# Four tiles of a normalised input transposed by DMA from ScalarE's queue in place of TensorE

## The chip, the core and the metric

The kernel runs on one core of a Trainium2 chip. The metric is the device time of one execution in microseconds (us). Engine names: PE is TensorE's matrix multiply and PEld its loading of weights, DVE is VectorE, ACT is ScalarE, POOL is GpSimd, SP is SyncE. SPq, ACTq and POOLq are the instruction streams from which these engines issue DMAs; each has a DMA queue of its own (in the DMA rows q1 is that of SP, q10 that of ACT, q0 that of POOL), and all of them use the same 16 DMA engines.

## What is computed

The input x has 2048 rows of 640 values in bf16. It is normalised row by row, and two branches of the normalised xn are added to x.

```
xn  = (x - mean(x)) / sqrt(var(x) + 1e-5)            # per row
q, k, v = xn @ wqkv                                  # 640 -> 3 x 640, 32 heads of 20
logits[s, w] = q[s] . k[s - 2 w] * 20**-0.5          # w = 0..7, masked where s - 2 w < 0
o   = softmax(logits) weighted sum of v[s - 2 w]
h   = (xn @ w_gate) * (xn @ w_up)                    # 640 -> 1536
out = x + o @ wo + h @ w_down
```

## The kernel before, in words

The rows are cut into 16 tiles of 128 rows, and four tiles make one of four chunks (`CH = 4`). In a chunk the matmuls take 512 rows at once. TensorE needs xn with the 640 features on the partitions, so each tile of xn is transposed once: `xnT` of a chunk is 128 x 5 x 512, with two buffers for the four chunks.

**Loading and normalising.** `load_x` (L163 to L167) loads one tile of x into one of five buffers. `ln` (L277 to L283) adds the steps of a tile: two halves of statistics on VectorE (L252), the mean and variance (L258, L260), the reciprocal root on GpSimd (L266), and the normalisation in place on VectorE (L271). The list `turn` in `ln` makes the statistics of tiles 0 to 4 wait for an earlier tile's normalisation, so that VectorE finishes tiles in turn there.

**Transposing.** `transposes` (L300 to L330) has two ways. Tiles under `XDMA = 8` are transposed by TensorE, five 128 x 128 blocks into PSUM (L310), and copied to xnT by ScalarE (L314). Tiles 8 to 15 are transposed by a DMA from SBUF to SBUF, issued by SP (L318). As soon as a tile is transposed, its buffer is free, so `transposes` also adds the load of x tile t + 5. Tiles 5 to 7 are loaded by SP, tiles 8 to 12 by ScalarE, tiles 13 to 15 by GpSimd.

**Products.** `qk` (L347 to L368) computes q and k of a chunk, ten groups of five matmuls of 128 x 512 (L355), each group in one PSUM bank that ScalarE evicts (L362). `vproj` computes v of one tile in two halves (L381, evicted at L387, stored at L398 to `vD` in DRAM). `load_v8` (L486) reads `vD` back with the eight shifted rows for each row. `prodlog` multiplies q with shifted k on VectorE, eight products of 128 x 2560 per chunk (L415) in five buffers, sums them by head on TensorE in two groups (L425), and evicts and transposes the logits (L438, L446, issued by SP). `softmax` and `av` are VectorE's (L460 to L527), and their output tile is transposed by an SP DMA (L534). `glu` computes gate and up (L551, evicted at L556, multiplied by VectorE at L567), `down` computes the output (L589, L592), added to x at L598.

**Order.** The kernel is planned before it is built. Each step is added with an engine, a cost in us and the steps it depends on. `Plan.order` walks all engines in time, and of the steps that are ready on an engine takes the one that is due first, counted back from the end. The result is one fixed list of instructions for each engine, and an engine does its list strictly in order. `after` is a dependence on the start of a step only, `occ` the time in which a step holds its engine, `floor` an earliest end, `margin` a delay added ahead of a step's start, and `kb` the size of a transfer that queues behind others on SP. The main matmuls, TensorE's transposes among them, form a chain through `pe_main` (L288 to L295): each comes after the one before, and after the eviction of the bank six places earlier (`ring`). The weights are loaded by SP in the order wv, wq, wk, wg, wu (`load`), then v of tile 0 and wd (`load_v8`, `load_down`).

At the place of the change, TensorE's order is written out by hand (L642 to L650): the five groups of q of chunk 0, the transposes of tiles 4 and 5, the five groups of k of chunk 0, the transposes of tiles 6 and 7, v of tile 3, and then (L673 to L676) q and k of chunk 1 and v of tiles 4 to 7. q and k of chunk 1 need `TT[4]` to `TT[7]`, the four tiles of chunk 1's xnT.

Of the kernel before, what the change touches and what calls it, by code (L numbers as in the profile page):

```python
# [9 lines left out]
ACT = mybir.ActivationFunctionType  # L10
# [21 lines left out]
class Plan:  # L32
# [8 lines left out]
    def add(self, eng, cost, fn, deps=(), occ=None, after=(), kb=0):  # L41
        s = Step(eng, cost, fn, deps, occ, after)
        s.kb = kb
        s.idx = len(self.steps)
        self.steps.append(s)
        return s
# [51 lines left out]
def kernel(  # L98
# [11 lines left out]
    nc = tc.nc  # L110
    P = nc.NUM_PARTITIONS
# [13 lines left out]
    NT = S // P  # L125
    CH = 4
# [27 lines left out]
    add = plan.add  # L154
    T = {}

    def new(key, shape, dtype, tag, bufs, pool=None):
        t = (pool or sb).tile(shape, dtype, name=tag, tag=tag, bufs=bufs)
        T[key] = t
        return t  # L160


    def load_x(t, eng=None):  # L163
        def fn():
            x = new(("x", t), [P, D], BF, "x", 5)
            (eng or nc.sync).dma_start(out=x[:], in_=x_flat[t * P : (t + 1) * P, :])  # L166
        return fn  # L167

    X = {}

    def wload(dst, src, eng=None):
        return lambda: (eng or nc.sync).dma_start(out=dst[:], in_=src.rearrange("(i p) f -> p i f", p=P))
# [9 lines left out]
    def load(at, fn, deps=()):  # L182
        s = chain[0] = add("SP", 2.0, fn, deps, occ=0.45, after=[chain[0]])
        s.floor = at
        return s
# [62 lines left out]
    def ln_stats(t, g):  # L248
        def fn():
            if g == 0:  # L250
                new(("st", t), [P, 2, nc.vector.BN_STATS_DIM], F32, "st", 3)
            nc.vector.bn_stats(T["st", t][:, g, :], T["x", t][:, g * NS : (g + 1) * NS])  # L252
        return fn

    def ln_aggr(t):
        def fn():
            mv = new(("mv", t), [P, nc.vector.BN_AGGR_DIM], F32, "mv", 6)
            nc.vector.bn_aggr(mv[:], T["st", t][:])  # L258
            ve = new(("ve", t), [P, 1], F32, "ve", 6)
            nc.vector.tensor_scalar(ve[:], mv[:, 1:2], scalar1=EPS, scalar2=None, op0=ALU.add)  # L260
        return fn

    def ln_rstd(t):
        def fn():
            rs = new(("rstd", t), [P, 1], F32, "rstd", 6)
            nc.gpsimd.tensor_tensor(rs[:], T["ve", t][:], mhalf[:], ALU.pow)  # L266
        return fn

    def ln_apply(t):
        def fn():  # L270
            nc.vector.tensor_scalar(T["x", t][:], T["x", t][:], scalar1=T["mv", t][:, 0:1],  # L271
                                    scalar2=T["rstd", t][:], op0=ALU.subtract, op1=ALU.mult)
        return fn

    XT, TT, GL, RS = {}, {}, {}, {}

    def ln(t):  # L277
        turn = [XT.get(t - (2 if t < CH else 1)), GL.get(t - 1)] if t <= CH else []
        a = add("DVE", 0.48, ln_stats(t, 0), [X[t], GL.get(t - 3), *turn], occ=0.395)
        a = add("DVE", 0.48, ln_stats(t, 1), [a], occ=0.395)  # L280
        a = GL[t] = add("DVE", 0.39, ln_aggr(t), [a], occ=0.3)
        b = RS[t] = add("POOL", 0.56, ln_rstd(t), [a])
        XT[t] = add("DVE", 0.443, ln_apply(t), [b], occ=0.35)  # L283
# [4 lines left out]
    def pe_main(cost, fn, deps=(), banks=1):  # L288
        nonlocal main
        waits = []  # L290
        for k in range(banks):
            if len(ring) + k >= 6:
                waits.append(ring[len(ring) + k - 6])
        main = add("PE", cost + 0.165, fn, [main, *waits, *deps], occ=cost)
        return main  # L295

    XDMA = 8
    GP = {}

    def transposes(t):  # L300
        c, q = divmod(t, CH)

        def slot():
            if q == 0:
                new(("xnT", c), [P, KT, CS], BF, "xnT", 2)

        def pe():
            ps = new(("pst", t), [P, KT, P], BF, "ps", 6, psum)
            for g in range(KT):
                nc.tensor.transpose(ps[:, g, :], T["x", t][:, g * P : (g + 1) * P], ident[:])  # L310

        def ev():
            slot()
            nc.scalar.copy(T["xnT", c][:, :, q * P : (q + 1) * P], T["pst", t][:])  # L314

        def dma():
            slot()
            nc.sync.dma_start_transpose(out=T["xnT", c][:, :, q * P : (q + 1) * P], in_=T["x", t][:])  # L318

        if t < XDMA:  # L320
            a = pe_main(0.28, pe, [XT[t]])
            TT[t] = add("ACT", 0.695, ev, [a], occ=0.6)
            ring.append(TT[t])
        else:
            a = TT[t] = add("SP", 2.8, dma, [XT[t], GP.get(c - 2)], occ=1.28, kb=200)
        if t + 5 < W:
            X[t + 5] = load(11.9 + 0.45 * t, load_x(t + 5), [a])
        elif t + 5 < NT:
            e, dge = ("ACT", nc.scalar) if t < XDMA else ("POOL", nc.gpsimd)
            X[t + 5] = add(e, 6.0, load_x(t + 5, dge), [a], occ=0.45, kb=0 if t < XDMA else 160)  # L330

    Q, Kk, LASTPW = {}, {}, {}
    HALOCP = {}

    def halo(c):
# [68 lines left out]
    SPLAST = [None]  # L404
    PW, LL, LE, SS, DD, AA, O16, OE, V8, DT = {}, {}, {}, {}, {}, {}, {}, {}, {}, {}

    def prodlog(c):
        for g in range(2):
            n = 2 * c + g
            for j in range(4):  # L410
                i = 4 * g + j

                def mul(i=i):
                    p = new(("pw", c, i), [P, KT, CS], BF, "pw", 5)
                    nc.vector.tensor_tensor(p[:], T["q", c][:], T["k", c][:, :, DIL * i : DIL * i + CS], ALU.mult)  # L415

                m = 8 * c + i
                PW[m] = add("DVE", 1.48, mul, [*Q[c], *Kk[c], LL.get((m - 5) // 4) if m >= 5 else None], occ=1.395)
            LASTPW[c] = PW[m]

            def lg(g=g):
                l = new(("lps", c, g), [P, 512], F32, "pl", 2, psum)
                for i in range(KT):
                    for j in range(4):
                        nc.tensor.matmul(l[H * j : H * (j + 1), :], lhsT=Ek[:, i, :], rhs=T["pw", c, 4 * g + j][:, i, :],  # L425
                                         start=(i == 0), stop=(i == KT - 1), tile_position=(0, H * j),
                                         skip_group_check=True)

            LL[n] = add("PE", 1.28, lg, [*[PW[8 * c + 4 * g + j] for j in range(4)], LE.get(n - 2), CE], occ=1.195)
            LL[n].urgent = True  # L430
            LL[n].margin = 1.0

            def ev(g=g):
                L = new(("L", c, g), [P, CS], BF, "L", 2)
                if c == 0:
                    ps = T["lps", c, g]
                    nc.vector.tensor_tensor(ps[:, 0:HALO], ps[:, 0:HALO], negm[:, g, :], ALU.add)
                nc.scalar.copy(L[:], T["lps", c, g][:])  # L438

            LE[n] = add("ACT", 0.585, ev, [LL[n], SS.get(n - 2), CM], occ=0.5)  # L440

            def tr(g=g):
                if g == 0:
                    new(("LT", c), [P, CH, W, H], BF, "LT", 1)
                out = T["LT", c][:].rearrange("p t (g w) h -> p t g (w h)", g=2)[:, :, g, :]
                nc.sync.dma_start_transpose(out=out, in_=T["L", c, g][:])  # L446

            early = [SPLAST[0]] if c == 0 else []
            SS[n] = SPLAST[0] = add("SP", 3.5, tr, [LE[n], DD.get(2 * c - 1), DD.get(2 * c - 2)], occ=1.25, after=early, kb=160)
            if c == 0 and g == 0:  # L450
                load_v8(1)
                SPLAST[0] = V8[1]
# [46 lines left out]
    def load_down():  # L499
        WL["d"] = SPLAST[0] = add("SP", 8, wload(wd, B_w_down), after=[SPLAST[0]], occ=0.5, kb=1920)  # L500

    def load_out():
        WL["o"] = SPLAST[0] = add("SP", 8, wo_load, after=[SPLAST[0]], occ=2.7, kb=1100)
# [121 lines left out]
    for t in range(4):  # L625
        ln(t)
# [3 lines left out]
    transposes(0)  # L630
    vproj(0, (0,))
    transposes(1)
    vproj(0, (1,))
    vproj(1, (0,))
# [5 lines left out]
    WL["g"] = load(17.2, wload(wg, B_w_gate))  # L640
    WL["u"] = load(23.2, wload(wu, B_w_up))
    qk(0, 0, CS, (0,))  # L642
    for t in (4, 5):
        ln(t)
        transposes(t)
    qk(0, 0, CS, (1,))
    for t in (6, 7):
        ln(t)
        transposes(t)
    vproj(3)  # L650
# [8 lines left out]
    def attention(c):  # L659
        if c == 0:  # L660
            SPLAST[0] = WL["u"]
            load_v8(0)
            load_down()
        prodlog(c)
        if c == 0:
            load_out()
            load_v8(2)
        for hf in range(2):
            softmax(c, hf)
        for q in range(CH):  # L670
            av(c * CH + q)
# [47 lines left out]
```

## Time and profile before

| | us |
|---|---|
| median of 3 runs | 269.42 (269.28 to 270.31) |
| the profiled execution | 269.1 |
| its span | 267.4 |
| PE busy | 260.2 (97%) |
| DVE busy | 215.2 (80%) |
| ACT busy | 108.6 (41%) |
| POOL busy | 40.7 (15%) |

The span runs from the first instruction to the last; 1.7 us of the profiled execution lie around it. Busy is the time in which an engine had at least one instruction of its own in work. A chain is followed back from the last instruction: at each step to what released it, or to the instruction before it on its engine. A row of a timeline gives the start, the length, the engine and line, what is written from what, how many instructions the row takes together, and in brackets the idle time ahead of it with what ended it. A row of DMA packets gives the queue, the number of packets, the megabytes, and the time of these packets as a share of the 16 DMA engines in the stretch that was asked for; packets in flight overlap, so a share can be over 100%. A landing is counted from the start of a DMA's issue.

### The profile page before, as it was taken

To read this page: it belongs to the slowest core of one execution; us is meant where nothing else is said; L and a number is where in the kernel's file an instruction comes from. 1 tells how busy PE (TensorE), PEld (TensorE's weight loads), DVE (VectorE), ACT (ScalarE), POOL (GpSimd) and SP (SyncE) were. 2 spreads that over 40 slices of the span, in tenths; PEclk is the share of its full clock that TensorE was granted. 3 is DMA by queue.
4 is the path that set the end of the run, shared out by engine and by line. 5 is a ranking of instruction groups with operands and counts; after the bars stand their busy time and mean duration, and the time that the engine had idled before them with its cause. 6 is when DMAs were issued, how large, how long until landed. Compare 5 with 4: busy or idle time off the path is not lost.

```text
span 267.4 us, 4130 instructions
## 1 busy us (share of the span) xinstructions
PE 260.2 (97%) x1596; PEld 141.7 (53%) x1596; DVE 215.2 (80%) x334; ACT 108.6 (41%) x197; POOL 40.7 (15%) x84
## 2 busy tenths in 40 slices
PE   7799999999999999999999999999999999999994
PEld 2545446444477645544456754644447764445772
DVE  4673999999999999999992999999829999931221
ACT  2657555655500066555520125655552005554000
POOL 4540006400003220500000010330000104000000
PEclk9999999999999999999999999999999999999999
DMA  6999977995497192995137947395029178110001
GB/s 217 356 390 398 367 186 248 252 232 146 110 285 173 44 319 101 241 343 81 25 61 103 298 170 222 89 331 50 20 45 368 57 241 150 25 25 0 27 31 43
DMA packets 47235, 45.89 MB, mean 172 GB/s; under 512 B 21954, under 2 KB 44368, under 8 KB 47216
## 3 DMA queue, kind: packets, MB, share of 16 engines
q1 hardware_dynamic: 43696, 36.28, 48.9%
q0 software_dynamic: 2384, 8.05, 9.4%
q10 hardware_dynamic: 1136, 1.31, 1.4%
q8 instruction: 12, 0.20, 0.4%
q14 instruction: 7, 0.06, 0.1%
HBM read 35.39 MB, written 5.26 MB: 152 GB/s over the span
## 4 chain that ended last, share of the span: by engine, by line
PE 95%; DMA 2%; ACT 1%; SPq 0%; issue 0%; DVE 0%; ACTq 0%
PE ps L551 39%; PE ps L589 20%; PE ps L355 16%; PE ps L592 8%; PE ps L381 8%; PE pl L425 4%; DMA wv<-in_A_wqkv_dram 2%; ACT xnT L314 1%; PE ps L310 0%; ACT v_t L387 0%; SPq L166 0%; DVE xr L598 0%; ACTq L166 0%; ACTq L387 0%
## 5 line engine op out<-in xcount | busy, mean ns | idle before, releaser
L551 PE MATMUL ps<-xnT,wg 128*128 128x512 bf16 x240 | 59.7, 379 | 0.0
L551 PE MATMUL ps<-xnT,wu 128*128 128x512 bf16 x240 | 59.7, 379 | 0.0
L589 PE MATMUL ps<-wd,hT 128*128 128x320 bf16 x384 | 57.4, 299 | 0.0
L415 DVE TENSOR_TENSOR pw<-q,k 128x2560 bf16<-128x2560 bf16 x32 | 46.4, 1485 | 2.2 <-ACT k L362 2.1
L589 PEld LDWEIGHTS <-hT 128*128 128x128 bf16 x384 | 37.4, 98 | 15.9 <-issue 0.8
L512 DVE TENSOR_TENSOR v<-v,a 128x5120 bf16<-128x5120 bf16 x16 | 45.1, 2819 | 0.1
L556 ACT CAST gs<-ps 128x512 bf16<-128x512 f32 x48 | 28.1, 586 | 40.7 <-PE ps L551 40.7
L551 PEld LDWEIGHTS <-wu 128*128 128x128 bf16 x240 | 23.3, 98 | 28.7 <-issue 0.8
L551 PEld LDWEIGHTS <-wg 128*128 128x128 bf16 x240 | 23.3, 98 | 28.1 <-issue 0.8
L556 ACT CAST us<-ps 128x512 bf16<-128x512 f32 x48 | 28.1, 586 | 23.3 <-PE ps L551 22.7
L567 DVE TENSOR_TENSOR hT<-gs,us 128x512 bf16<-128x512 bf16 x48 | 19.8, 420 | 14.4 <-ACT us L556 14.2
L598 DVE TENSOR_TENSOR xr<-ps,xr 128x320 bf16<-128x320 f32 x32 | 14.8, 485 | 19.4 <-PE ps L592 15.6
L592 PE MATMUL ps<-wo,oT 128*128 128x320 bf16 x160 | 27.0, 299 | 0.0
L620 POOL DMA_DIRECT2D out_dram<-xr x14 | 7.7, 548 | 123.0 <-DVE xr L598 123.0
L381 PE MATMUL ps<-wv,xnT 128*128 128x320 bf16 x160 | 23.6, 299 | 1.4 <-DMA wv<-in_A_wqkv_dram 1.1
L521 DVE TENSOR_TENSOR v<-v 128x2560 bf16<-128x2560 bf16 x16 | 23.8, 1485 | 0.1
L355 PE MATMUL ps<-xnT,wq 128*128 128x512 bf16 x100 | 22.2, 379 | 0.2 <-ACT xnT L314 0.2
L355 PE MATMUL ps<-xnT,wk 128*128 128x512 bf16 x100 | 22.4, 379 | 0.0
L381 PEld LDWEIGHTS <-xnT 128*128 128x128 bf16 x160 | 15.2, 98 | 8.5 <-ACT xnT L314 1.9
L592 PEld LDWEIGHTS <-oT 128*128 128x128 bf16 x160 | 15.7, 98 | 6.1
L252 DVE BATCH_NORM_STATS2 st<-x 128x6 f32<-128x320 bf16 x32 | 13.8, 481 | 6.3 <-DMA x<-in_A_x_dram 6.3
L362 ACT CAST q<-ps 128x512 bf16<-128x512 f32 x20 | 11.7, 586 | 17.2 <-PE ps L355 17.2
(52 smaller groups left out, 183.9 us busy)
## 6 DMA issues: line engine op xcount, KB each, us to landing
v<-vD SPq DMA_DIRECT2D x16, 1280.0 KB, 6.8
vD<-v_t POOLq DMA_DIRECT2D x16, 160.0 KB, 4.6
xr<-in_A_x_dram POOLq DMA_DIRECT2D x16, 160.0 KB, 5.9
out_dram<-xr POOLq DMA_DIRECT2D x14, 160.0 KB, 2.9
wg<-in_B_w_gate_dram SPq DMA_DIRECT2D x1, 1920.0 KB, 10.7
wu<-in_B_w_up_dram SPq DMA_DIRECT2D x1, 1920.0 KB, 15.9
wd<-in_B_w_down_dram SPq DMA_DIRECT2D x1, 1920.0 KB, 20.8
x<-in_A_x_dram SPq DMA_DIRECT2D x7, 160.0 KB, 5.0
```

The lines of the kernel that those rows point to most:

```text
L252: nc.vector.bn_stats(T["st", t][:, g, :], T["x", t][:, g * NS : (g + 1) * NS])
L355: nc.tensor.matmul(ps[:, 0:n], lhsT=(wk if r else wq)[:, i, j * P : (j + 1) * P], rhs=T["xnT", c][:, i, lo : lo + n], start=(i == 0), stop ...
L381: nc.tensor.matmul(ps[:, 0:NS], lhsT=T["xnT", c][:, i, q * P : (q + 1) * P], rhs=wv[:, i, n * NS : (n + 1) * NS], start=(i == 0), stop=(i ...
L415: nc.vector.tensor_tensor(p[:], T["q", c][:], T["k", c][:, :, DIL * i : DIL * i + CS], ALU.mult)
L512: nc.vector.tensor_tensor(v[:].rearrange("p w (j h) -> p w j h", j=Dh, h=H), v[:].rearrange("p w (j h) -> p w j h", j=Dh, h=H), T["a", n][ ...
L521: nc.vector.tensor_tensor(v[:, 0:4, :], v[:, 0:4, :], v[:, 4:8, :], ALU.add)
L551: nc.tensor.matmul(ps[:], lhsT=(wu if r else wg)[:, i, f * P : (f + 1) * P], rhs=T["xnT", c][:, i, :], start=(i == 0), stop=(i == KT - 1))
L556: nc.scalar.copy(s[:], T[key][:])
L567: nc.vector.tensor_tensor(h[:], T["gs", c, f][:], T["us", c, f][:], ALU.mult)
L589: nc.tensor.matmul(ps[:, 0:NS], lhsT=T["hT", c, f][:, q * P : (q + 1) * P], rhs=wd[:, f, sl], start=(f == 0), stop=(f == FT - 1 and not wo ...
L592: nc.tensor.matmul(ps[:, 0:NS], lhsT=T["oT", t][:, g, :], rhs=wo[:, g, sl], start=False, stop=(g == KT - 1 and f1 == FT))
L598: nc.vector.tensor_tensor(T["xr", t][:, sl], T["psD", t, n][:, 0:NS], T["xr", t][:, sl], ALU.add)
```

## The change

Tiles 4 to 7 are transposed by DMA as tiles 8 to 15 are, but issued by ScalarE. In ScalarE's list the issue of tile 4 stands behind the eviction of q's first group of chunk 0, that of tile 5 behind the second, tile 6 behind the fourth and tile 7 behind the fifth (`behind`), and the ten evictions of q and k of chunk 0 are held in order. The planner counts 4.5 us for such a transpose, 1.28 us of it on ScalarE. TensorE's transposes of these tiles and ScalarE's copies are gone. `turn` now covers tiles 0 to 7, so that the statistics of tile t wait for the normalisation of tile t - 2 (for tile 4: of tile 3). The loads of x tiles 9 to 12 move from ScalarE to SP, behind wd; tile 8 stays with ScalarE.

```
@@ -273,9 +273,14 @@
         return fn
 
     XT, TT, GL, RS = {}, {}, {}, {}
+    Q, Kk, LASTPW = {}, {}, {}
+
+    def behind(s, a):
+        s.after.append(a)
+        s.deps.append(a)
 
     def ln(t):
-        turn = [XT.get(t - (2 if t < CH else 1)), GL.get(t - 1)] if t <= CH else []
+        turn = [XT.get(t - (1 if t == CH else 2)), GL.get(t - 1)] if t < 2 * CH else []
         a = add("DVE", 0.48, ln_stats(t, 0), [X[t], GL.get(t - 3), *turn], occ=0.395)
         a = add("DVE", 0.48, ln_stats(t, 1), [a], occ=0.395)
         a = GL[t] = add("DVE", 0.39, ln_aggr(t), [a], occ=0.3)
@@ -294,7 +299,7 @@
         main = add("PE", cost + 0.165, fn, [main, *waits, *deps], occ=cost)
         return main
 
-    XDMA = 8
+    XDMA = 4
     GP = {}
 
     def transposes(t):
@@ -315,21 +320,25 @@
 
         def dma():
             slot()
-            nc.sync.dma_start_transpose(out=T["xnT", c][:, :, q * P : (q + 1) * P], in_=T["x", t][:])
+            (nc.sync if c > 1 else nc.scalar).dma_start_transpose(out=T["xnT", c][:, :, q * P : (q + 1) * P], in_=T["x", t][:])
 
         if t < XDMA:
             a = pe_main(0.28, pe, [XT[t]])
             TT[t] = add("ACT", 0.695, ev, [a], occ=0.6)
             ring.append(TT[t])
         else:
-            a = TT[t] = add("SP", 2.8, dma, [XT[t], GP.get(c - 2)], occ=1.28, kb=200)
+            e, cost, kb = ("SP", 2.8, 200) if c > 1 else ("ACT", 4.5, 0)
+            a = TT[t] = add(e, cost, dma, [XT[t], GP.get(c - 2)], occ=1.28, kb=kb)
+            if c == 1:
+                a.margin = 0.5
+                behind(a, (Q[0] + Kk[0])[(0, 1, 3, 4)[q]])
         if t + 5 < W:
             X[t + 5] = load(11.9 + 0.45 * t, load_x(t + 5), [a])
-        elif t + 5 < NT:
-            e, dge = ("ACT", nc.scalar) if t < XDMA else ("POOL", nc.gpsimd)
-            X[t + 5] = add(e, 6.0, load_x(t + 5, dge), [a], occ=0.45, kb=0 if t < XDMA else 160)
-
-    Q, Kk, LASTPW = {}, {}, {}
+        elif t == 3:
+            X[t + 5] = add("ACT", 6.0, load_x(t + 5, nc.scalar), [a], occ=0.45)
+        elif 8 <= t < NT - 5:
+            X[t + 5] = add("POOL", 6.0, load_x(t + 5, nc.gpsimd), [a], occ=0.45, kb=160)
+
     HALOCP = {}
 
     def halo(c):
@@ -640,11 +649,10 @@
     WL["g"] = load(17.2, wload(wg, B_w_gate))
     WL["u"] = load(23.2, wload(wu, B_w_up))
     qk(0, 0, CS, (0,))
-    for t in (4, 5):
-        ln(t)
-        transposes(t)
     qk(0, 0, CS, (1,))
-    for t in (6, 7):
+    for a, b in zip(Q[0] + Kk[0], (Q[0] + Kk[0])[1:]):
+        behind(b, a)
+    for t in range(CH, 2 * CH):
         ln(t)
         transposes(t)
     vproj(3)
@@ -661,6 +669,8 @@
             SPLAST[0] = WL["u"]
             load_v8(0)
             load_down()
+            for t in range(9, 13):
+                X[t] = SPLAST[0] = add("SP", 2.3, load_x(t), [TT[t - 5]], after=[SPLAST[0]], occ=0.5, kb=160)
         prodlog(c)
         if c == 0:
             load_out()
```

More of the change, by code (lines that the diff above doesn't have):

```diff
@@ L275, with behind @@
     XT, TT, GL, RS = {}, {}, {}, {}
+    Q, Kk, LASTPW = {}, {}, {}
+    def behind(s, a):
+        s.after.append(a)
+        s.deps.append(a)
     def ln(t):
-        turn = [XT.get(t - (2 if t < CH else 1)), GL.get(t - 1)] if t <= CH else []
+        turn = [XT.get(t - (1 if t == CH else 2)), GL.get(t - 1)] if t < 2 * CH else []
         a = add("DVE", 0.48, ln_stats(t, 0), [X[t], GL.get(t - 3), *turn], occ=0.395)
@@ L295, in pe_main @@
         return main
-    XDMA = 8
+    XDMA = 4
     GP = {}
@@ L317, in dma @@
             slot()
-            nc.sync.dma_start_transpose(out=T["xnT", c][:, :, q * P : (q + 1) * P], in_=T["x", t][:])
+            (nc.sync if c > 1 else nc.scalar).dma_start_transpose(out=T["xnT", c][:, :, q * P : (q + 1) * P], in_=T["x", t][:])
         if t < XDMA:
@@ L324, in transposes @@
         else:
-            a = TT[t] = add("SP", 2.8, dma, [XT[t], GP.get(c - 2)], occ=1.28, kb=200)
+            e, cost, kb = ("SP", 2.8, 200) if c > 1 else ("ACT", 4.5, 0)
+            a = TT[t] = add(e, cost, dma, [XT[t], GP.get(c - 2)], occ=1.28, kb=kb)
+            if c == 1:
+                a.margin = 0.5
+                behind(a, (Q[0] + Kk[0])[(0, 1, 3, 4)[q]])
         if t + 5 < W:
             X[t + 5] = load(11.9 + 0.45 * t, load_x(t + 5), [a])
[L328 to L332, printed above, removed]
+        elif t == 3:
+            X[t + 5] = add("ACT", 6.0, load_x(t + 5, nc.scalar), [a], occ=0.45)
+        elif 8 <= t < NT - 5:
+            X[t + 5] = add("POOL", 6.0, load_x(t + 5, nc.gpsimd), [a], occ=0.45, kb=160)
     HALOCP = {}
@@ L642 @@
     qk(0, 0, CS, (0,))
-    for t in (4, 5):
-        ln(t)
-        transposes(t)
     qk(0, 0, CS, (1,))
-    for t in (6, 7):
+    for a, b in zip(Q[0] + Kk[0], (Q[0] + Kk[0])[1:]):
+        behind(b, a)
+    for t in range(CH, 2 * CH):
         ln(t)
@@ L663, in attention @@
             load_down()
+            for t in range(9, 13):
+                X[t] = SPLAST[0] = add("SP", 2.3, load_x(t), [TT[t - 5]], after=[SPLAST[0]], occ=0.5, kb=160)
         prodlog(c)
```

## The prediction

> **What bounds the kernel now.** I read the page from its first part, then the chain of waits, then the start of the kernel engine by engine, and last the DMA packets queue by queue.
>
> ```profile
> PE 260.2 (97%) x1596; PEld 141.7 (53%) x1596; DVE 215.2 (80%) x334; ACT 108.6 (41%) x197; POOL 40.7 (15%) x84
> ...
> PE 95%; DMA 2%; ACT 1%; SPq 0%; issue 0%; DVE 0%; ACTq 0%
> ```
>
> TensorE is busy for 97% of the span, and 95% of the chain that ended last is its own work. So a microsecond taken from TensorE's list counts, and so does one in which it has nothing to do: no idle time stands later that could take it in. The stage that the change touches is this, in TensorE's timeline:
>
> ```profile
> 13.69 5.56 PE L355 MATMUL ps<-xnT,wq 128*128 128x512 bf16 x25 [0.20 <-ACT xnT L314]
> 19.08 0.72 PE L310 MATMUL ps<-ident,x 128*128 128x128 bf16 x10
> 19.64 5.56 PE L355 MATMUL ps<-xnT,wk 128*128 128x512 bf16 x25
> 25.04 0.72 PE L310 MATMUL ps<-ident,x 128*128 128x128 bf16 x10
> 25.59 1.52 PE L381 MATMUL ps<-wv,xnT 128*128 128x320 bf16 x10
> ```
>
> The columns are start, length, instruction. The two rows of L310 are the transposes of tiles 4 to 7. Each pushes its successor back by 0.55 us (19.64 - 13.69 less 25 matmuls of 0.216). At 27.07 follow the matmuls of chunk 1's q, which need all four transposed tiles.
>
> **Removed from TensorE.** Two pairs of transposes: 2 x 0.55 = **-1.1 us**. Without any wait chunk 1's q would start at 27.07 - 1.1 = 25.97. That is the most the change can bring, 0.4% of the time; a measurement of this kernel tells about 0.5% from no change.
>
> **ScalarE.** Four copies of L314 go (1.29 + 1.30 = 2.6 us) and four x loads (about 0.37 each, 1.5); four transpose issues come (1.21 to 1.27 each on SP's queue, 5.1). Net 1.0 us; from 13.7 to 27.07 ScalarE is busy 8.47 of 13.37 us, which hides it. Behind each issue wait evictions (0.59 each, one per 1.08 us): each issue overlaps the eviction before it and sets the next back by some 0.7 us, so they fall at most two banks behind in a ring of six: nothing. Without that cover TensorE would wait for a bank, about 0.7 us per issue. The issues then fall at about 15.3 (tile 4 is normalised at 15.25), 17.2, 19.3 and 20.7.
>
> **SyncE, VectorE, GpSimd.** SP's four x loads (0.35 to 0.52 each) fall behind wd's issue, which ends at 23.67; its next instruction before was L446 at 36.05, so the issues are free, but each waits for its tile's transpose to land, and L446 waits behind them. VectorE does the same work; the new turn touches only tiles 5 to 7, normalised from 15.96 to 19.13 before, and each is ready when ScalarE gets to it: nothing. GpSimd's work is the same, its stores wait for evictions that move by under 1 us.
>
> **The transposes as transfers** decide. TensorE waits for the last of the four. Before, no transpose of this size ran on ScalarE's queue, so its landing must be worked out from neighbours. Alone it is quick: in the DMA view from 124 to 132 us the packets of one are
>
> ```profile
> q1 hardware_dynamic: 672, 0.16, 10.6%
> ```
>
> (queue, packets, MB, share of the 16 engines). 10.6% of 8 us is 0.85 us, with packets of 256 bytes: 16 x 0.85/672 = 0.020 us of one engine for each; 640 packets a tile are 40 on each engine, 160 for four tiles. But from 13.7 to 35 us the DMA engines are full with wg, wu, v and wd from SP's queue. The DMA view of single microseconds, 22 to 23, 25 to 26, 28 to 29:
>
> ```profile
> q1 hardware_dynamic: 138, 0.42, 104.9%
> ```
> ```profile
> q1 hardware_dynamic: 150, 0.19, 55.7%
> q10 hardware_dynamic: 149, 0.17, 50.0%
> ```
> ```profile
> q1 hardware_dynamic: 289, 0.37, 107.5%
> ```
>
> SP's queue (q1) moves 138 packets of 3 KB in one microsecond (16/138 = 0.116 us each on an engine), later 289 of 1280 bytes (0.055). When ScalarE's queue (q10) has x tiles to load, the two take turns **one packet for one packet**: 150 to 149. A transpose has packets of 256 bytes, so it would get one small packet for each large one. That this holds for transposes too is seen once, on SP's queue against GpSimd's (q0) from 177.9 to 178.4 us:
>
> ```profile
> q0 software_dynamic: 51, 0.18, 97.5%
> q1 hardware_dynamic: 56, 0.03, 17.9%
> ```
>
> 51 packets of 3.5 KB beside 56 of the transpose. The view of 173 to 175 has its landing:
>
> ```profile
> oT<-o SPq DMA_TRANSPOSE x1, 10.1
> ```
>
> Issued at 173.59, behind v's packets on its own queue too, that tile took 10.1 us to land, against 2.6 alone.
>
> The sum. First packets come late: x tile 9, issued at 20.98, shows none before 24, tile 8 (12.91) few before 17. So tile 4, issued at 15.3, starts at about 19.0, and the others queue behind it. From 19 to 24.7 SP's queue still had about 45 packets of 3 KB per engine: 45 turns x (0.116 + 0.020) = 6.1 us, to 25.1. The other 115 turns go against the 1280-byte packets of v and wd: 115 x 0.075 = 8.6 us, to 33.7. Some engine is always late (x tile 10 landed 1 us after its bulk, wd 3 us): I take 1.5. Tile 7 lands at **35.2**, TensorE goes on at 35.3 in place of 27.07: **+8.2 us**, the saved 1.1 included.
>
> Bounds: at best each lands as the one at 114.37 (3.9 us beside GpSimd's queue), tile 7 at 24.6, no wait, -1.1. At worst the last lands when all is drained: wd's 39.1, less 1.7 for the four x tiles now behind it (0.43 each), plus 4 x 0.85: 40.8, +13.8. I take the value by packets, since the row nearest in time and queue is that of 25 to 26.
>
> [...]
>
> **A second term, TensorE's start after 9 us of nothing.** The trace shows one start after idle, the warm-up: 12 matmuls of 128x512.
>
> ```profile
> 1.45 4.23 PE L243 MATMUL ps<-gs,ident 128*128 128x512 bf16 x12 [1.45 <-POOL ident masks.py:199]
> ```
>
> The first seven follow each other by 0.43 us, against 0.216 later: 7 x 0.21 = 1.5 us lost. After a wait of 9 us I take **+1.5**; no row shows such a wait in mid-kernel, so 0 to 1.5 stays in the range. [...]
>
> **Sum.** 269.1 + 8.2 + 1.5 = 278.8 for the profiled execution (span 267.4 and 1.7 around it), 0.3 below the median shown; I say **279.0**. VectorE idles with TensorE: its fifth product of 1.4 us ends near 32.3, and the next needs the logits matmuls, six groups after the wait, near 43. It is as late as TensorE, so nothing else becomes late. Case range: 272.6 (packets that cost SP's nothing: 45 x 0.116 + 115 x 0.055 from 19 gives 30.5, no tail, no slow start) to 284.4 (40.8 and 1.5).
>
> **Rivals.** *On time* (not slower): the landing is like 3.9 us under load, or turns are by bytes or larger packets. It decides at 25.97: landing there or before gives -1.1, **268.0**, about 268.3 against the median; at 27.07 nothing is won. For it: the tile at 114.37. Against: that tile's packets came only after GpSimd's were done. Chance 0.12.
>
> *A little late*: equal shares by bytes, 0.85 x 2 a tile after 3.5 us of delay: tile 7, issued at 20.7, lands near 28; **270** (269 to 272.6). Chance 0.08.
>
> *VectorE held by tile 9*: the transposes are on time, but tiles 9 to 11 come behind wd, at 39.1 - 1.7 + 3.4 + 0.4 = 41.2, and their statistics, 2.45 us in the gap at 32.87 before, stand after the eighth product, done near 38.1. VectorE waits 3 us there and reaches the softmax about 1.5 us late (49.0 for 47.53), TensorE being 1.1 early. Output tile 2's transpose landed at 82.3 and was used at 83.95: slack 1.65 against 2.6, so 0.95 of the gain is lost: **269.0**. Chance 0.06.
>
> **Chances.** Late by packets 0.74, slower by over 0.5% throughout. Faster by over 0.5% would need 1.35 us, more than is removed: 0.04 of on time, for a wait elsewhere that I don't see. Within: most of on time and held, part of a little late. 269 to 284 leaves out on time and the tails.
>
> **To look for.** Right: TensorE idle from about 26 to 35, ended by the DMA of xnT; in 20 to 25 us as many packets of q10 as of q1; landings of 9 us and more; 0.43 us matmuls after it. Wrong: landings near 4 to 5 us, no wait of TensorE before q's second chunk.

## The result, and the profile after

The changed kernel takes 280.99 us (280.86 to 281.75), the kernel before 269.42: the ratio is 1.0441, with a 95% interval from 1.0421 to 1.0461. The profiled execution of after took 281.75 us with a span of 280.0, so 12.65 us more than that of before (269.1); it is 0.8 us longer than the other three. Line numbers have moved by five to ten lines: L364 is the q and k matmul (L355 before), L390 v's, L323 the transposing DMA, L371 the eviction of q and k.

From the page of after, engine busy time and the chain that ended last:

```profile
PE 261.9 (94%) x1558; PEld 141.6 (51%) x1576; DVE 215.4 (77%) x334; ACT 106.1 (38%) x193; POOL 42.1 (15%) x84
...
PE 86%; DMA 9%; issue 2%; ACT 1%; SPq 0%; DVE 0%; ACTq 0%
```

TensorE's own share of the chain fell from 95% to 86%; what came in is DMA, from 2% to 9%. TensorE's timeline of after, in the stretch that the prediction showed:

```profile
19.06 5.56 PE L364 MATMUL ps<-xnT,wk 128*128 128x512 bf16 x25
24.45 0.84 PE L390 MATMUL ps<-wv,xnT 128*128 128x320 bf16 x5
29.58 1.49 PE L390 MATMUL ps<-wv,xnT 128*128 128x320 bf16 x5 [4.28 <-ACT k L371]
37.27 0.59 PE L364 MATMUL ps<-xnT,wq 128*128 128x512 bf16 x1 [6.20 <-DMA xnT<-x]
38.08 7.43 PE L364 MATMUL ps<-xnT,wq 128*128 128x512 bf16 x23 [0.22 <-issue]
45.34 1.24 PE L364 MATMUL ps<-xnT,wk 128*128 128x512 bf16 x5
```

The transposes are gone and k starts at 19.06 in place of 19.64. Then TensorE stands still twice: 4.28 us until ScalarE frees a bank, and 6.20 us until the last transpose lands. Chunk 1's q starts at 37.27 in place of 27.07 (+10.2), and its 25 matmuls take 8.07 us in place of 5.39 (+2.7). 10.2 + 2.7 = 12.9; by the end 0.2 of it is won back. The packets of the DMA queues in two single microseconds of after, 25 to 26 and 35 to 36:

```profile
q1 hardware_dynamic: 119, 0.37, 91.9%
q10 hardware_dynamic: 119, 0.03, 13.4%
```
```profile
q1 hardware_dynamic: 244, 0.31, 84.0%
q10 hardware_dynamic: 243, 0.06, 27.3%
```

In 25 to 26 there are 119 packets of 3 KB of the weights to 119 packets of 256 bytes of the transposes: 0.37 MB against 0.03. Later there are 244 packets of 1280 bytes to 243. The four tiles, issued at 15.01, 17.16, 19.47 and 25.11, took 12.2, 14.1, 14.6 and 11.9 us to land; the last landed at 37.0. ScalarE's own stream in that time:

```profile
15.01 1.47 ACTq L323 DMA_TRANSPOSE xnT<-x  x1
...
17.16 2.17 ACTq L323 DMA_TRANSPOSE xnT<-x  x1
...
19.47 5.54 ACTq L323 DMA_TRANSPOSE xnT<-x  x1
...
25.11 3.79 ACTq L323 DMA_TRANSPOSE xnT<-x  x1
28.94 2.54 ACT L371 CAST k<-ps 128x512 bf16<-128x512 f32 x5 [8.50 <-issue]
```

The third and fourth issue take 5.54 and 3.79 us, where 1.2 to 1.3 was expected, and k's five evictions run only after them. That is TensorE's first stop, and TensorE's clock changes in it. In the rows below the granted clock is the number ahead of the last two: it falls from 1.00 to 0.50 inside this first stop, at 29.1, and rises again only at 42.7, within chunk 1's q.

```profile
29.00:29.50 0.50, 0.00 (x0) 0.00 (x0) 0.00 (x0) 0.50 (x2) 0.00 (x0) 0.57 1.14 381
42.50:43.00 0.50, 0.50 (x4) 0.13 (x2) 0.00 (x0) 0.00 (x0) 0.00 (x0) 0.77 0.00 0
```

### The profile page after: what moved, and what is told of

It is laid out like the page before. It is cut to its first block, busy times and chain, and to the rows that moved or that the text cites. A ratio compares the mean times of both kernels' runs of the same rounds, so it can differ in the third digit from the quotient of the medians.

```text
span 280.0 us, 4071 instructions
## 1 busy us (share of the span) xinstructions
PE 261.9 (94%) x1558; PEld 141.6 (51%) x1576; DVE 215.4 (77%) x334; ACT 106.1 (38%) x193; POOL 42.1 (15%) x84
## 4 chain that ended last, share of the span: by engine, by line
PE 86%; DMA 9%; issue 2%; ACT 1%; SPq 0%; DVE 0%; ACTq 0%
PE ps L560 37%; PE ps L598 19%; PE ps L364 12%; PE ps L601 8%; PE ps L390 7%; DMA xnT<-x 4%; PE pl L434 3%; DMA x<-in_A_x_dram 3%; DMA wv<-in_A_wqkv_dram 2%; ACT xnT L319 0%; ACT v_t L396 0%; SPq L166 0%; DVE xr L607 0%; ACTq L396 0%; ACTq L323 0%
## 5 line engine op out<-in xcount | busy, mean ns | idle before, releaser
L560 PE MATMUL ps<-xnT,wg 128*128 128x512 bf16 x228 | 59.0, 379 | 0.6
L565 ACT CAST gs<-ps 128x512 bf16<-128x512 f32 x48 | 28.1, 586 | 35.2 <-PE ps L560 35.2
L560 PEld LDWEIGHTS <-wu 128*128 128x128 bf16 x240 | 23.5, 98 | 28.3
L364 PE MATMUL ps<-xnT,wq 128*128 128x512 bf16 x96 | 24.7, 410 | 6.8 <-DMA xnT<-x 6.2
L390 PE MATMUL ps<-wv,xnT 128*128 128x320 bf16 x160 | 24.4, 304 | 5.7 <-ACT k L371 4.3
L364 PE MATMUL ps<-xnT,wk 128*128 128x512 bf16 x98 | 22.3, 379 | 0.1
L390 PEld LDWEIGHTS <-xnT 128*128 128x128 bf16 x160 | 15.4, 99 | 13.5 <-issue 5.2
L371 ACT CAST q<-ps 128x512 bf16<-128x512 f32 x20 | 11.6, 586 | 24.9 <-PE ps L364 23.9
L364 PEld LDWEIGHTS <-wq 128*128 128x128 bf16 x100 | 10.3, 104 | 20.4 <-issue 11.1
```

The costliest lines, as they stand in the source:

```text
L364: nc.tensor.matmul(ps[:, 0:n], lhsT=(wk if r else wq)[:, i, j * P : (j + 1) * P], rhs=T["xnT", c][:, i, lo : lo + n], start=(i == 0), stop ...
L390: nc.tensor.matmul(ps[:, 0:NS], lhsT=T["xnT", c][:, i, q * P : (q + 1) * P], rhs=wv[:, i, n * NS : (n + 1) * NS], start=(i == 0), stop=(i ...
L560: nc.tensor.matmul(ps[:], lhsT=(wu if r else wg)[:, i, f * P : (f + 1) * P], rhs=T["xnT", c][:, i, :], start=(i == 0), stop=(i == KT - 1))
L565: nc.scalar.copy(s[:], T[key][:])
```

## The experiments

The theory is that of the prediction: the queues take turns packet for packet, so small packets starve beside large ones. The rivals are that a transpose from ScalarE's queue is slow of itself, that bytes or time are shared (so packet sizes don't matter), that ScalarE's blocked evictions are what costs, and that the loss lies in the rest of the change. Each ratio is to the kernel before on the same chip. In the code shown, ... stands for lines left out.

**wu held back.** SP issues wu, and so v and wd, only behind a small DMA that reads tile 7's part of xnT (the planner's earliest end for the load of v moves with it, from 30.5 to 35.5).

```
+    def wu_held():
+        nc.sync.dma_start(out=seen[:], in_=T["xnT", 1][0:1, 0, 3 * P : 4 * P])
+        nc.sync.dma_start(out=wu[:], in_=B_w_up.rearrange("(i p) f -> p i f", p=P))
+    WL["u"] = load(31.0, wu_held, [TT[7]])      # in place of load(23.2, wload(wu, B_w_up))
```

> The changed kernel, with one thing moved: SP issues wu (and behind it v and wd) only after a small DMA that reads tile 7's part of xnT, so after tile 7's transpose has landed. While the four transposes run, only the rest of wg competes. Turns packet for packet: wg ends near 20 us, the four tiles then run alone, tile 7 lands by about 25, TensorE goes on to chunk 1 at 26 to 27 without a wait of microseconds and without slow matmuls: 268 to 270.5 us. Rival, a transpose from ScalarE's queue is slow of itself: landings stay at 12 to 14 us, TensorE waits to about 37, 280 us or more. Rival, ScalarE's queue is full after two tiles whatever else runs: its third and fourth issue still take 4 to 5 us each and hold the evictions.

Measured: 269.78 us, ratio to before 1.0011 (0.9986 to 1.0036). The four landings are 7.6, 6.0, 4.5 and under 3.8 us, chunk 1's q starts at 26.09 without a wait, and its 25 matmuls take 5.4 us. ScalarE's issues take 1.4, 1.3 and 1.6 each: it is not full after two tiles when they can drain. So the transpose is not slow of itself; what ran beside it made it slow. But TensorE's 1.0 us does not reach the end. Its waits in this kernel have a line that before lacks (wait, total, times, longest):

```profile
PE ps L602 <- DMA oT<-o: 2.7, 2, 1.5
```

From 24.1 to 26.0 us the DMA engines were almost idle (20 packets of SP's queue), and SP's loads came later; the second logits transpose landed at 51.1 in place of 47.1, VectorE began the softmax at 51.16 in place of 47.53, and TensorE waited for output tiles 2 and 3.

**The same bytes in smaller packets.** wg and wu are each loaded in four column slices, 768 bytes a packet in place of 3072.

```
+            for j in range(4):
+                f = slice(j * F // 4, (j + 1) * F // 4)
+                nc.sync.dma_start(out=dst[:, :, f], in_=src[:, f].rearrange("(i p) f -> p i f", p=P))
```

> The changed kernel with wg and wu loaded in four column slices each: the same bytes from the same queue, in packets of 768 bytes in place of 3072. Turns packet for packet: a turn costs about 0.034 + 0.020 us in place of 0.134, so the four tiles' packets flow at about 270 per us from the start (120 per us in the changed kernel up to 28 us), the last lands at 30 to 31 in place of 37, and the time falls to 274 to 276 us. Shares by bytes or by time: the size of the others' packets doesn't matter, landing near 37 and 280 to 282 us. Slow of itself: the same, 280 to 282 us.

Measured: 275.61 us, 1.0207 (1.017 to 1.0245). The bytes and their order on the queue are the same, and 5.4 of the 11.6 us are back. In 24 to 25 us:

```profile
q1 hardware_dynamic: 336, 0.25, 76.4%
q10 hardware_dynamic: 336, 0.09, 38.5%
```

336 to 336, again one for one; the transposes' share of the bytes went from 0.03 to 0.09 MB. Tile 7's wait ended at 31.3. This tells packets from bytes. One thing more differs: SP has eight loads to issue in place of two, so it issues v at 24.88 and wd at 27.32, 7.0 and 4.7 us later. Both stand behind wu on the same queue, which still had packets of 768 bytes to send until about 31, so the transposes were never without them beside.

**TensorE kept at work in the wait.** 20 matmuls of zeros before chunk 1's q; their result is not used.

```
+    def busy():
+        ps = psum.tile([P, 512], F32, name="ps", tag="ps", bufs=6)
+        for _ in range(20):
+            nc.tensor.matmul(ps[:], lhsT=ident[:], rhs=T["wz"][:], start=True, stop=True)
+    main = add("PE", 4.4, busy, [main])
```

> The changed kernel with 20 matmuls of zeros (128x512, result not used) on TensorE between v of tile 3 and chunk 1's q, that is in its wait for xnT. Slow start after idleness: the 25 matmuls of chunk 1's first q take 5.4 us in place of 8.1, the profile's clock shows no more 0.74 there, and the time falls by 2 to 3 us to 278 to 279. Rival, the slow matmuls after the wait come from something else (DMA traffic, weight loads): no change, 281 us. If the 20 run slowly to the end they reach 39.7 and add up to 2.5 us.

Measured: 278.33 us, 1.0317 (1.0276 to 1.0357): 2.7 us less than the changed kernel, though TensorE does more. The added matmuls begin at 29.12 and are slow themselves from 29.9 to 33.3 (a granted clock of 0.50), but inside the wait, where it costs nothing. From 35 to 50 us the granted clock (ahead of the last two numbers) of the changed kernel and of this one:

```profile
35.00:50.00 15.00, 12.46 (x59) 5.05 (x62) 5.79 (x6) 4.69 (x8) 0.00 (x0) 0.74 0.42 141
```
```profile
35.00:50.00 15.00, 13.37 (x90) 5.56 (x91) 12.19 (x25) 6.44 (x11) 1.75 (x3) 1.00 0.69 228
```

0.74 against 1.00. The last transpose lands about where it did (TensorE resumes at 36.81, 0.46 earlier) and the same transfers run beside it, so in these two runs the slow matmuls go with TensorE's standing idle, and not with the DMA traffic.

**Issued behind the evictions.** All four transposes stand in ScalarE's list behind the last eviction of chunk 0's k.

```
-                behind(a, (Q[0] + Kk[0])[(0, 1, 3, 4)[q]])
+                behind(a, TT[t - 1] if q else Kk[0][4])
```

> The changed kernel with all four transposes issued by ScalarE only behind the last eviction of chunk 0's k, near 25 us, so that no issue stands ahead of an eviction. Turns packet for packet: TensorE no longer waits for a bank (4.3 us at 25.3 in the changed kernel), but xnT lands no earlier: first packets near 28.5, some 90 turns against v and wd to 34.5, the rest alone, landing 37 to 38, 280 to 282 us. Rival, the blocked evictions are what costs: with them free the time falls to 271 to 273 us.

Measured, in a single execution: 284.55 us. No eviction waits, VectorE begins its products at 25.08 in place of 31.52, and TensorE stands still for xnT until 39.67, 2.4 us later than in the changed kernel. So the blocked evictions were not what cost: that wait lay inside the wait for xnT. The time is above what I expected, since I had the landing 2 us too early: from 36 to 38 the transposes ran almost alone and yet at only some 240 packets per us (247 from 36 to 37), where the run with wu held back shows 924 (from 22 to 23). Why is not known.

**The rest of the change alone.** Turn and x tiles 9 to 12 as in the change, the four tiles transposed by TensorE (XDMA = 8).

> The kernel before with the rest of the change and without its transposes: tiles 4 to 7 still by TensorE, the turn up to tile 7, x tiles 9 to 12 loaded by SP behind wd. No wait of TensorE near 26; x tile 9 lands by about 38, the statistics of tiles 9 to 11 leave the gap at 32.9 and stand behind the eighth product, near 39, and VectorE comes up to 2.4 us later to the output tiles, against a slack of 1.65: 269.4 to 270.5 us. If the rest carried the change's loss it would be 275 or more.

Measured: 269.38 us, 0.9998 (0.9978 to 1.0018). The rest costs nothing without the transposes; the loss comes with them. VectorE did the statistics at 39.33, without a wait.

**The transposes on SP's queue, between wg and wu.**

```
-            (nc.sync if c > 1 else nc.scalar).dma_start_transpose(...)
+            nc.sync.dma_start_transpose(...)
...
+                behind(a, TT[t - 1] if q else WL["g"])
...
+    chain[0] = TT[7]
+    WL["u"] = load(27.0, wload(wu, B_w_up))
```

> The changed kernel with the four transposes issued by SP, on the queue of the weights, between wg and wu: they stand in line behind wg and nothing takes turns with them but a few of GpSimd's packets. Turns packet for packet: issued from 15 to 20 us, each lands within 3 to 6 us, all by 24, TensorE starts chunk 1's q near 26 without a wait and without slow matmuls. The logits transposes come 1 to 3 us later through the same queue, so part of the 1.0 us won is given back at the output tiles: 268.3 to 270 us. If a transpose between 14 and 36 us is slow on any queue: landings of 10 us or more, over 275.

Measured: 271.23 us, 1.0068 (1.004 to 1.0095). In line behind wg the four land in 8.0 to 2.6 us, TensorE starts chunk 1's q at 25.70, and no matmul is slow. Yet the whole is slower than before: the price of VectorE's lateness is larger than TensorE's gain. VectorE waits 2.73 us for x tile 9 (landing at 40.7 behind wd), and the second logits transpose lands at 48.7. In the profiled execution TensorE then waits not for the output tiles, as I had expected, but ahead of them for VectorE's product of gate and up (hT), 1.11 and 0.23 us. That execution took 270.16 us, one of the shortest of the twelve (270.02 to 273.05), so it does not show all of the loss.

**wd behind the logits transposes**, on top of that run:

```
-            load_down()                       # ahead of x tiles 9 to 12 and prodlog
         prodlog(c)
         if c == 0:
+            load_down()
             load_out()
```

> The run with the transposes on SP's queue, with wd moved behind the second logits transpose, so that x tiles 9 to 12 and the logits transposes don't stand behind it. If what eats TensorE's gain is VectorE coming late to the output tiles (tile 9 to 11's statistics and the logits transposes behind wd), TensorE's 1.1 us stays: 268.2 to 268.6 us. If not, as the run without it.

Measured: 271.29 us, 1.006 (1.0038 to 1.0083): a miss. The planner now thought x tile 9 early and put its statistics ahead of the sixth product, and the tile landed at 35.8:

```profile
35.81 1.83 DVE L252 BATCH_NORM_STATS2 st<-x 128x6 f32<-128x320 bf16 x4 [3.02 <-DMA x<-in_A_x_dram]
```

VectorE waits 3.02 us there, with the products behind it, and TensorE 1.4 us for the products.

**The same order of loads with TensorE's transposes** (the run with the rest alone, with wd moved as above):

> The same order of loads (x tiles 9 to 12 on SP, wd behind the second logits transpose), with tiles 4 to 7 still transposed by TensorE. TensorE has nothing less to do: 269.2 to 269.8 us, 1 us above the run with the transposes on SP's queue if that one wins by its 1.1 us of TensorE's time.

Measured: 269.75 us, 1.0019 (0.9996 to 1.0042). The order alone brings nothing.

**x tiles 9 to 12 by GpSimd**, wd late, transposes on SP's queue, and the planner told of their landing:

```
-        elif 8 <= t < NT - 5:
+        elif t < NT - 5:
             X[t + 5] = add("POOL", 6.0, load_x(t + 5, nc.gpsimd), [a], ...)
...
+                a.floor = 21.3 + 0.6 * q
```

> The run with the transposes on SP's queue and wd late, with x tiles 9 to 12 loaded by GpSimd, so that they don't stand behind the weights, and with the planner told when the four transposes land (21.3 to 23.1 in its time). If VectorE's wait for x tile 9 and the late logits are what ate the 1.1 us, tile 9 and 10's statistics go back into the gap near 32, VectorE does not wait for x, TensorE does not wait at the output tiles: 268.2 to 268.8 us. If something else eats it: 269.5 to 271.

Measured: **268.20 us, 0.9969 (0.9942 to 0.9995)** against 269.28 of before on that chip: the only version of the study that beats the kernel before, by 1.1 us (0.1 to 1.6 by the interval, so just clear of noise), the amount of TensorE's work removed. VectorE's statistics of tiles 9 and 10 are back in the gap and the softmax starts early, from VectorE's timeline:

```profile
32.09 1.67 DVE L252 BATCH_NORM_STATS2 st<-x 128x6 f32<-128x320 bf16 x4
...
45.93 0.28 DVE L469 TENSOR_TENSOR m<-LT 128x256 bf16<-128x256 bf16 x1
```

45.93 in place of 47.53 before. TensorE has no wait later than 14 us.

**The same with wd ahead of the logits transposes:**

> As the run before it, but with wd left ahead of the logits transposes. The second logits transpose then lands 1 to 2 us later than in the kernel before (47.1): 268.3 to 269.6 us, by how far that late landing uses up the slack at the output tiles.

Measured: 271.48 us, 1.0076 (1.0046 to 1.0106), a miss on the slow side. Only wd's place differs, and VectorE's row of the softmax shows it:

```profile
48.49 0.29 DVE L469 TENSOR_TENSOR m<-LT 128x256 bf16<-128x256 bf16 x1 [2.35 <-DMA LT<-L]
```

The second logits transpose landed at 48.4, behind the load of v, which had itself stood behind wd. 2.6 us of lateness there cost 3.3 at the end by the medians (2.5 by the profiled executions).

## Why the prediction was right, step by step

**Removed from TensorE, -1.1: right.** Chunk 1's q starts 1.0 to 1.4 us earlier wherever nothing holds it (26.09 and 25.70 for 27.07); counted from the start of chunk 0's q it is 1.2 in both.

**The transposes as transfers: right in mechanism, 1.8 us short in size.** The turns are one packet for one packet, 119 to 119 where the sum had 16/0.136 = 118, and 244 to 243 where it had 16/0.075 = 213. The start at 19.0 held (70 packets of q10 in 19 to 20, of which some are x tile 8's). Tile 7 landed at 37.0 and not at 35.2. What the sum lacked are two stretches, 20 to 22 and 27 to 29, in which both queues moved at about half their pace (55 and 49, then 122 and 82 packets of q1); in each they nearly stop, from 20.5 to 21.5 and from 27.7 to 28.3. They show in the run with small packets and the one with matmuls of zeros too, at 20 and at 26 or so; their cause wasn't found and stays open. In these three runs a packet of an instruction queue (q8 or q14; here at 19.3 and 27.0) stands 0.7 to 1.3 us ahead of each, and in the kernel before the same packets come at 19.1 and 26.7, with no transposes in flight, and nothing stops (124 packets of q1 from 20.3 to 21.3, 281 from 27 to 28). That is a candidate and no more: the run with the issues behind the evictions has a stop of 0.3 us at 29.4, just after its transposes' first packets, with no such packet near.

Part of the agreement is luck. The two stretches alone cost about 2.2 us, an estimate from the packets that are missing in them (128 of q10 at 119 per us, 283 at 243). Two terms of the sum were too large and hid that: a turn against the 1280-byte packets took 16/243 = 0.066 us and not 0.075, 1.0 us less over 115 turns, and the last tile landed 0.7 us after its last bulk of packets (36.3) where 1.5 was set. These three don't add up to the 1.8; in 19 to 20 there were 34 packets of GpSimd's queue as well, and the rest stays open.

Equal counts over half a microsecond or a whole one, as in the prediction and above, don't show how long a turn is: if both queues sent the same number of packets in a turn, however many, 119 would stand beside 119 as well. Finer stretches of after show it, 22.10 to 22.18 and 22.24 to 22.30:

```profile
q1 hardware_dynamic: 17, 0.05, 154.6%
q10 hardware_dynamic: 17, 0.00, 23.9%
```
```profile
q1 hardware_dynamic: 16, 0.05, 204.0%
q10 hardware_dynamic: 16, 0.00, 30.0%
```

Between the two no packet starts, and 22.36 to 22.44 has 16 and 16 again. A packet of q1 takes about 0.12 us there and one of q10 0.02 (154.6% and 23.9% of 16 x 0.08 us, over 17 packets each), so one packet of each fills an engine for the 0.13 us from one group to the next, the length of one turn in the sum. The 16 engines then send one packet of each queue per engine in a turn: an estimate from these rows, which don't name the engine of a packet.

**The slow start, 1.5: mis-sized, 2.7.** The mechanism is shown by the run with zeros, which takes 2.7 us off. I had the length from the warm-up at the kernel's start, seven matmuls at half speed; in after the evictions of chunk 1's q stand at 39.60, 41.73, 43.38 and 44.47, so the slow pace lasts for more than two groups of five. The granted clock, taken in slices of 0.1 us, shows how long it lasts (at the kernel's start it can't be read so: there the rows give 1.00 though the first seven matmuls follow each other by 0.43 us, against 0.216 later). It falls and rises at 29.08 and 42.73 in after, at 29.53 and 36.35 with small packets, at 29.91 and 33.32 with the matmuls of zeros, at 29.94 and 43.60 with the issues behind the evictions: 13.65, 6.82, 3.41 and 13.66 us apart, that is 4, 2, 1 and 4 times 3.41. In these runs, then, the clock changes only on steps of 3.41 us, and after the restart at 37.27 TensorE stayed slow until such a step came, for 5.5 us (with small packets for 5.0).

In after the clock fell inside the stop of 4.28 us, with small packets inside one of 5.59 us. With the matmuls of zeros it fell after a gap of 2.83 us, and with the issues behind the evictions after gaps of 1.03 us at most, with a matmul of 0.38 us between them; yet a gap of 1.53 us, in the run with zeros, brought no fall. So the length of the gap alone does not tell these cases apart. What these four falls share is a step of 3.41 us in which TensorE worked little: 0.00, 0.00, 0.74 and 1.13 us of it. A step with 1.96 us of work, in the run with zeros, left the clock at 1.00. Whether it is the work in a step that decides, and where between 1.13 and 1.96 us the limit would then lie, no run shows.

**ScalarE, nothing: wrong.** I had each issue at 1.2 us beside an eviction. Two of them took 5.54 and 3.79 us while the queue drained slowly (1.4, 1.3 and 1.6 each in the run with wu held back, where it drained faster), and TensorE stood 4.28 us for a bank. The stop itself cost nothing here only since it ended at 29.6, before the transposes landed; the run with the issues behind the evictions shows that removing it wins nothing.

**VectorE as late as TensorE: right.** It idled until 47.8, and the shift of 12.9 us at chunk 1's q is 12.65 at the end.

**The rival "VectorE held by tile 9"** did not decide the changed kernel, but both runs with the transposes on SP's queue and x tiles 9 to 12 behind them met it (waits of 2.73 and 3.02 us for x tile 9), at a higher price than the 0.95 us I gave it: some 3 us each against the 268.2 of the run in which GpSimd loads these tiles. In the first of them, and in the run with wu held back, a late logits transpose came on top or in its place.

Sum: 8.2 + 1.5 was forecast, 10.2 + 2.7 measured, both terms in the direction that was said.

## What to carry to other kernels

In this kernel a transfer of small packets on a second queue did not share the DMA engines evenly by bytes with one of large packets (0.03 MB beside 0.37 from 25 to 26, 119 packets beside 119). In such a place price it as its number of packets per engine times the time of one packet of each queue, not by its bytes, and allow for stretches in which neither moves (here 20.5 to 21.5 and 27.7 to 28.3). If it is needed soon, put it in line on the same queue ahead of what can wait (here landings of 8.0 to 2.6 us), or hold the other queue back (7.6 to under 3.8); then follow everything behind it on that queue, since the time that it takes there is paid by whoever waits next. And TensorE's wait of 6.20 us cost more than its length here: the slow restart behind it took another 2.7 us.

## What the runs showed of the hardware that was not expected

The issue of a DMA can wait, as if its queue were full, and holds its engine's whole list: in after two issues took 5.54 and 3.79 us, and k's five evictions began only at 28.94. The third issue ended near 25.0, when about 32 of the 120 packets per engine so far issued had gone (519 packets of q10 from 19.5 to 25, over 16 engines), the fourth at 28.9 with about 58 of 160 gone: some 90 to 100 packets per engine seem to fit, an estimate from these two times. In the run with the issues behind the evictions the fourth ended at 33.0 with about 56 of 160 gone, which agrees. The slow pace after TensorE's stops (2.7 us lost) was longer than that at the kernel's start (1.5 us), and in the four runs in which the granted clock fell it changed only on steps of 3.41 us.
